# Attention and a gated MLP on one core: the sums of a pair of heads transposed two units later

## The chip, the cores and the metric

The kernel runs on one core of a Trainium2 chip. The metric is device time in microseconds (us) of the whole kernel; lower is better. TensorE (PE) multiplies and transposes; VectorE (DVE), ScalarE (ACT) and GpSimd (POOL) work on elements; SyncE (SP) issues the transfers. Each engine carries out its own list of instructions in order, and semaphores between the engines say when an instruction may start.

## The reference, cut to what matters

```python
def _attn_ref(q, k, v):                       # 4 batches, 8 heads, 576 rows, 64 columns
    scores = scale * np.matmul(q, k.transpose(0, 1, 3, 2))
    mask = block_i >= block_j                 # blocks of 64 rows
    scores = np.where(mask, scores, -1000000000.0)
    scores = scores - np.max(scores, axis=-1, keepdims=True)
    attn = np.exp(scores)
    attn = attn / (np.sum(attn, axis=-1, keepdims=True) + 1e-09)
    return np.matmul(attn, v)
def _moe_ref(x, w_in, w_spatial, b_spatial, w_out):
    h = np.maximum(x @ w_in, 0.0)
    u, v = (h[..., :d_ff // 2], h[..., d_ff // 2:])
    v_n = (v - mu) / np.sqrt(var + 1e-06)     # mean and variance of v's rows
    v_s = np.einsum('ts,bsd->btd', w_spatial, v_n) + b_spatial[None, :, None]
    return (u * v_s) @ w_out
def _moe2_ref(x, g_ln, w_ch1, w_ch2):
    xn = (x - mu) / np.sqrt(var + 1e-06) * g_ln
    return x + np.maximum(xn @ w_ch1, 0.0) @ w_ch2
```

The output of the attention goes through the gated MLP and then through the second MLP, which adds its input.

## The kernel before

**Pairs and units.** The 4 x 8 heads are taken as 16 pairs of heads of one batch, numbered from 0; four pairs make a batch. A pair is worked off in nine units (UNITS). Unit 0 is the tail: the last 64 query rows of both heads, which see all 576 keys. Units 1 and 2 are the fourth block of 128 query rows of each head (four blocks of keys), units 3 and 4 the third (three), 5 and 6 the second (two), 7 and 8 the first (one).

**A unit.** scores(u) multiplies q and k on PE into a bank of the pool p_sc (rows L268 to L308 of the profile). softmax(u) takes the masked maximum on DVE (L323, with L327 for the tail's two parts) and the exponential on ACT (L330), which adds up each row's sum into a column of the tile sm. Two units later (D = 2) transposes(u) turns the unnormalized weights p by 128 x 128 blocks on PE (L380, "tr", as many as there are blocks of keys; the tail has five, in two banks) into a bank of the pool p_tr, which has **two** banks. put copies them to the tiles pH (units of three and four blocks and the tail; by DVE L372, some three-block ones by ACT L374) or pL (the small units; by ACT L374). A bank of p_tr is free for the next taker when this copy is done.

**A pair's end.** Because of the two units' delay, the end of pair p-1 lies in the first units of pair p. At i == 0, unit 7 of p-1 is transposed and reciprocals(p - 1) follows; at i == 1 unit 8; at i == 2 the tail of p itself, and weighted(p - 1, 0), the product of pL with v (L431, "pv<-pL") in a bank of the pool p_mm, which has three. The product with pH, weighted(p, 1), comes in the pair itself at i == 7. reciprocals adds 1e-9 to the sums (L340, DVE), inverts them (L341, DVE), transposes the 128 x 9 tile to nine rows (L343, PE, "rps", a bank of p_tr), copies it (L345, ACT, "rr") and sends it to DRAM and back spread over 64 partitions each ("rb", SP's transfers). store_x, at i == 5, multiplies xx, the copy of the products, by rb (L441, POOL) and splits the result into a high and a low part, xT (L60, L444).

**What else runs there.** While the pairs run, decode_in prepares the MLP's weights (L88 ACT; L89, L90 DVE; L101, L102 POOL, "win"), and prepare casts and splits the next pair's q and k (L58 ACT; L243, L245 POOL, "stack"). From the fifth pair on, fill puts matmuls of the first MLP for finished batches between the units: the value half ("vps", L106 to L108, followed by ACT's vr and DVE's BN_STATS, L112) and the gate half ("ups"). The written order is not the final one: a scheduler reorders each engine's list when the program is built, by its own estimate of the times.

After attention (from about 280 us) come the mixing over rows, the output product and the second MLP, which the change doesn't touch.

Of the kernel before, what the change touches and what calls it, by code (L numbers as in the profile page):

```python
# [8 lines left out]
F32 = mybir.dt.float32  # L9
# [24 lines left out]
def tile_kernel(  # L34
# [26 lines left out]
    NB, NP, _, _, _, S = qk.shape  # L61
# [7 lines left out]
    NPAIR = NB * NP  # L69
# [62 lines left out]
    p_mm = tc.alloc_tile_pool(name="p_mm", bufs=PLAN["mm"], space=PSUM, side="left")  # L132
    p_sc = tc.alloc_tile_pool(name="p_sc", bufs=PLAN["sc"], space=PSUM, side="right")
    p_tr = tc.alloc_tile_pool(name="p_tr", bufs=PLAN["tr"], space=PSUM, side="right")
# [12 lines left out]
    def load(p):  # L147
        if p >= NPAIR:
            return
        b, hp = divmod(p, NP)  # L150
        if p >= PACKED or p % 2 == 0:
            both[:] = [at.tile([128, 2, 2, S], F32, tag="qkt", name="qkt")]
        raw = both[0] if p >= PACKED else both[0][:, p % 2:p % 2 + 1]
        for half in range(2):
            rows = slice(64 * half, 64 * half + 64)
            for j in (0,) if p < PACKED else range(2):
                for x in range(2):
                    h = half if p < PACKED else j
                    nc.sync.dma_start(out=raw[rows, j, x], in_=qk[b, hp, :, h, x])
        nat[p] = raw  # L160

    def load_v(p):
        if p >= NPAIR:
            return
        vts[p] = at.tile([128, 5, 128], F32, tag="vt", name="vt", bufs=3)
        last_load[:] = [nc.sync.dma_start(out=vts[p], in_=v[divmod(p, NP)])]
# [8 lines left out]
    def warm(n):  # L175
        for _ in range(n):
            pin(MM(idle, lhsT=zeros.to_broadcast([128, 128]), rhs=zeros.to_broadcast([128, 512]), start=True, stop=True))
# [136 lines left out]
    def softmax(u):  # L314

        j, c = UNITS[u % NU]
        banks = state[u]
        sm = sums[u // NU]
        pt = tail if c == 4 else at.tile([128, 512], F32, tag="p", name="p", bufs=PLAN['pt'])
        nm = at.tile([128, 2], F32, tag="nm", name="nm", bufs=4)  # L320
        for i, (s_ps, o, n) in enumerate(banks):
            m = mask[:, 0:n] if c == 4 else mask[:, 512 - n:512]
            nc.vector.tensor_tensor_reduce(  # L323
                pt[:, o:o + n], s_ps[:, :n], m, -0.125, 3e38, ALU.add, ALU.min, nm[:, i:i + 1]
            )
        if c == 4:
            nc.vector.tensor_tensor(nm[:, 0:1], nm[:, 0:1], nm[:, 1:2], op=ALU.min)  # L327
        n = o + n
        col = 8 if c == 4 else 4 * j + c
        nc.scalar.activation(  # L330
            pt[:, :n], pt[:, :n], AF.Exp, bias=nm[:, 0:1], scale=-1.0, accum_out=sm[:, col:col + 1]
        )
        state[u] = (pt, n)
# [3 lines left out]
    def reciprocals(p):  # L337

        sm = sums.pop(p)
        nc.vector.tensor_scalar(sm, sm, 1e-9, None, op0=ALU.add)  # L340
        nc.vector.reciprocal(sm, sm)  # L341
        ps = p_tr.tile([128, 512], F32, tag="tr", name="rps")
        nc.tensor.transpose(ps[:9, :128], sm, idn)  # L343
        rr = at.tile([128, 128], F32, tag="rr", name="rr", bufs=1)
        (nc.vector.tensor_copy if p == NPAIR - 1 else nc.scalar.copy)(rr[:9], ps[:9, :128])  # L345
        nc.sync.dma_start(out=r_d[p, :, 0:512].rearrange("j (c q) -> j c q", q=128), in_=rr[:8])
        nc.sync.dma_start(out=r_d[p, :, 512:S], in_=rr[8:9])
        rb = at.tile([128, S], F32, tag="rb", name="rb")
        for j in range(2):
            nc.sync.dma_start(out=rb[64 * j:64 * j + 64], in_=r_d[p, j].partition_broadcast(64))  # L350
        rb_t[p] = rb
# [13 lines left out]
    def transposes(u):  # L365
        j, c = UNITS[u % NU]
        pt, n = state.pop(u)

        def put(src, dst):
            out = dst(pT_of(u // NU)[1 if c >= 2 else 0])  # L370
            if u >= NS - NU or c >= PLAN["ev1" if u >= NU * NP else "ev0"] and not (c == 4 and PLAN["tl1" if u >= NU * NP else "tl0"] == "s"):
                nc.vector.tensor_copy(out, src)  # L372
            else:
                nc.scalar.copy(out, src)  # L374

        def flip(k0, k1):
            tr = p_tr.tile([128, 512], F32, tag="tr", name="tr")
            for kc in range(k0, k1):
                o = 128 * (kc - k0)
                nc.tensor.transpose(tr[:, o:o + 128], pt[:, 128 * kc:128 * kc + 128], idn)  # L380
            return tr

        if c == 4:
            tr = flip(0, 4)
            put(
                tr.rearrange("p (r h q) -> p r h q", h=2, q=64),
                lambda t: view(t, 256, [[WH, 4], [5 * WH, 2], [1, 64]]),
            )
            tr = flip(4, 5)
            put(tr[:, 0:128].rearrange("p (h q) -> p h q", q=64), lambda t: t[:, :, 4 * WH + 256:5 * WH])  # L390
        else:
            tr = flip(0, c + 1)
            put(
                tr[:, :n].rearrange("p (r q) -> p r q", q=128),
                lambda t: view(
                    t, (5 * WH if c >= 2 else 2 * WL) * j + 128 * (c % 2), [[WH if c >= 2 else WL, c + 1], [1, 128]]
                ),
            )
# [5 lines left out]
    def tick():  # L404
        for e in list(slow):
            e[0] -= 1
            if e[0] <= 0:
                slow.remove(e)
                e[1]()

    def flush():
        todo, later[:] = list(later), []
        for f in todo:
            f()

    def weighted(p, part):

        flush()
        vt = ops[p][2]
        if p not in xx_t:  # L420
            xx_t[p] = at.tile([128, S], F32, tag="xx", name="xx")
        xx = xx_t[p]

        jobs = ((0, 128, 0, WL), (1, 128, 128, WL)) if part == 0 else (
            (0, 128, 0, WH), (1, 128, 0, WH), (2, 128, 0, WH), (3, 128, 128, WH), (4, 128, 256, WH))
        w = WH if part else WL
        src = pT_of(p)[part]
        ps = p_mm.tile([128, 512], F32, tag="mm", name="pv")
        for n, (kc, rows, a, z) in enumerate(jobs):
            for j in (1, 0):  # L430
                MM(  # L431
                    ps[64 * j:64 * j + 64, a:z], lhsT=vt[:rows, kc, 64 * j:64 * j + 64],
                    rhs=src[:rows, j, w * kc + a:w * kc + z],
                    start=(n == 0), stop=(n == len(jobs) - 1),
                )
        later.append(lambda: cp('xe', None, xx[:, 256 * part:256 * part + w], ps[:, :w]))

    def store_x(p):
        b, hp = divmod(p, NP)
        xx = xx_t.pop(p)  # L440
        E('xm', p).tensor_tensor(xx, xx, rb_t.pop(p), op=ALU.mult)  # L441
        c0 = (b % 2) * S
        cp('xh', p, xT[0][:, hp, c0:c0 + S], xx)
        E('xl', p).tensor_tensor(xT[1][:, hp, c0:c0 + S], xx, f32(xT[0][:, hp, c0:c0 + S]), op=ALU.subtract)  # L444
        del ops[p]
# [112 lines left out]
    D = PLAN['D']  # L558
    WARM = {2: 5, 3: 2, 4: 2, 5: 1}
    DECODE = {1, 7, 12, 17, 22, 38, 42, 46, 50}  # L560
    for u in range(NS + 8):
        p, i = divmod(u, NU)
        if u < NS:
            scores(u)
            warm(WARM.get(u, 0))
            softmax(u)
        tick()
        flush()
        if D <= u < NS + D:
            transposes(u - D)  # L570
        if i == PLAN['wd'] and p < NPAIR:
            weighted(p, 1)
        if i == 0 and 1 <= p <= NPAIR:
            reciprocals(p - 1)
        if i == D and 1 <= p <= NPAIR:
            weighted(p - 1, 0)
        if i == D + 3 and 1 <= p <= NPAIR:
            store_x(p - 1)
        if i == 0:
            for q in range(2, PACKED) if p == 0 else range(max(p + 2, PACKED), p + 3):  # L580
                load(q)
            load_v(p + 2)
            if p + 1 < NPAIR:
                preps[0] = prepare(p + 1)
        if 0 in preps and i >= 1:
            next(preps[0], None)
        if u in DECODE:
            next(dec, None)
        if p >= NP:
            b, k = divmod(u, NU * NP)  # L590
            if b == 1 and k < 2:
                if k == 0:
                    ahead_of_x = w_in_stage(0)
                next(ahead_of_x)
            if k == PLAN['dstart'] and b <= NB - 1:
                dense = chain(dense, ahead_of_x if b == 1 else w_in_stage(b - 1))
            fill(PLAN['rate'] * size[i] / tot)
# [592 lines left out]
```

## Time and profile before

| | |
|---|---|
| time, median of 3 runs | 803.19 us (801.56 to 804.18) |
| profiled execution, its own time | 804.05 us |
| its span | 802.3 us |
| busy: PE / DVE / ACT / POOL | 98% / 65% / 53% / 52% |
| PE's share of the chain that ended last | 87% |

The span runs from the first to the last instruction of the profiled execution; its own time is 1.75 us longer. A share is that of the whole span. An engine that is busy 98% of it can hardly have more than 2% taken from its waits.

### The profile page before, as it was taken

What the parts mean: (1) busy time and instruction counts of PE and PEld (TensorE: products, weight loads), DVE (VectorE), ACT (ScalarE), POOL (GpSimd) and SP (SyncE); (2) the same over time, 40 slices, a digit from 0 to 9 for tenths busy, and PEclk for the clock granted to TensorE, in tenths of its full rate; (3) what the DMA queues carried; (4) which work ended last, traced back from release to release, by engine and by line L of the source; (5) the groups of instructions that cost most, each with busy time, mean ns of one, the idle gap of its engine ahead of it and who ended that gap; (6) DMA issues with size and microseconds to landing.
All of it is one profiled execution on the core that took longest, in us unless ns stands there. A gap on an engine that the chain in (4) does not pass through costs nothing.

```text
span 802.3 us, 13325 instructions
## 1 busy us (share of the span) xinstructions
PE 782.6 (98%) x4504; PEld 669.7 (83%) x4508; DVE 521.3 (65%) x1184; ACT 428.6 (53%) x1080; POOL 418.5 (52%) x435
## 2 busy tenths in 40 slices
PE   9989899999999999999999999999999999999998
PEld 4667688878888799889988889888889888888986
DVE  6667655665555277877677787897566588645534
ACT  4776677677675264555354554553354454433421
POOL 4598865765462352233285465555545465445431
PEclk9999999999999999999999999999999999999999
DMA  9855454446242468788420342204001003000002
GB/s 253 194 154 166 125 158 137 123 142 189 67 150 73 139 211 279 224 265 279 160 93 1 102 135 79 80 0 158 1 21 34 0 1 125 21 1 1 1 1 78
DMA packets 53848, 88.70 MB, mean 111 GB/s; under 512 B 6931, under 2 KB 17299, under 8 KB 53781
## 3 DMA queue, kind: packets, MB, share of 16 engines
q1 hardware_dynamic: 53540, 87.55, 36.4%
q8 instruction: 35, 0.57, 0.3%
q10 hardware_dynamic: 240, 0.31, 0.2%
q14 instruction: 33, 0.26, 0.1%
HBM read 68.88 MB, written 18.95 MB: 109 GB/s over the span
## 4 chain that ended last, share of the span: by engine, by line
PE 87%; DVE 6%; DMA 3%; ACT 2%; issue 1%; POOL 1%; SPq 0%; POOLq 0%; DVEq 0%; ACTq 0%
PE hps L969 21%; PE o L106 8%; PE o L108 8%; PE o L107 8%; PE pv L431 6%; PE tr L380 5%; PE sc L308 4%; PE ups L106 2%; PE ups L108 2%; PE ups L107 2%; PE vps L106 2%; DMA raw<-in_w_ch_dram 2%; PE vps L107 2%; PE vps L108 2%; PE sc L302 2%; PE sc L286 2%
## 5 line engine op out<-in xcount | busy, mean ns | idle before, releaser
L102 POOL TENSOR_TENSOR a<-s,a 128x256 fp32r<-128x256 f32 x96 | 78.3, 820 | 93.0 <-ACT a L97 93.0
L107 PE MATMUL o<-w,h 128*128 128x512 f32 x288 | 112.9, 393 | 0.0
L106 PE MATMUL o<-w,h 128*128 128x512 f32 x288 | 107.8, 398 | 1.0 <-ACT h L961 1.0
L975 DVE TENSOR_TENSOR c<-hps,c 128x384 f32<-128x384 f32 x120 | 66.5, 554 | 54.6 <-PE hps L969 53.0
L108 PE MATMUL o<-w,h 128*128 128x512 f32 x288 | 97.5, 397 | 0.1
L323 DVE CUSTOM_DVE_ANT_0 p<-sc,mask 128x512 f32<-128x512 f32 (+3 forms) x128 | 58.5, 478 | 50.5 <-PE sc L308 27.0
L330 ACT ACTIVATE p<-p,nm 128x512 f32<-128x512 f32 (+3 forms) x128 | 71.1, 556 | 28.7 <-DVE nm L323 27.6
L102 POOL TENSOR_TENSOR a<-w,a 128x256 fp32r<-128x256 f32 x72 | 61.0, 850 | 44.4 <-ACT a L97 38.6
L97 ACT CAST a<-s 128x256 fp32r<-128x256 f32 x96 | 38.4, 404 | 84.3 <-PE hps L969 76.1
L372 DVE COPY pH<-tr 128x512 f32<-128x512 f32 (+1 forms) x88 | 49.6, 574 | 32.8 <-PE tr L380 32.1
L106 PEld LDWEIGHTS o<-w,h 128*128 128x128 f32 x288 | 53.7, 188 | 11.8 <-ACT h L961 2.3
L107 PEld LDWEIGHTS o<-w,h 128*128 128x128 f32 x288 | 54.1, 188 | 10.1
L108 PEld LDWEIGHTS o<-w,h 128*128 128x128 f32 x288 | 53.2, 188 | 8.8 <-DVE h L962 1.0
L380 PE MATMUL tr<-idn,p 128*128 128x128 f32 x320 | 55.0, 279 | 4.2 <-DVE pH L372 4.0
L819 POOL TENSOR_TENSOR gt<-gf,gt 128x576 fp32r<-128x576 f32 (+1 forms) x17 | 25.0, 1471 | 61.1 <-ACT gt L818 61.1
L380 PEld LDWEIGHTS tr<-idn,p 128*128 128x128 f32 x320 | 37.7, 140 | 14.2 <-DVE pH L372 6.2
L117 POOL TENSOR_TENSOR rs<-rs,nhalf 128x1 f32<-128x1 f32 x36 | 22.4, 623 | 49.4 <-DVE rs L116 44.4
L962 DVE SCALAR_TENSOR_TENSOR h<-c,h 128x384 fp32r<-128x384 f32 x72 | 46.5, 665 | 1.5 <-ACT h L961 1.5
L243 POOL TENSOR_TENSOR stack<-qkt,stack 64x576 fp32r<-64x576 f32 x24 | 34.5, 1439 | 23.5 <-ACT stack L58 19.2
L88 ACT ACTIVATE dm<-raw 128x256 f32<-128x256 f32 (+1 forms) x72 | 32.1, 462 | 26.9 <-DVE w L90 9.2
L308 PE MATMUL sc<-stack 128*128 128x512 f32 (+3 forms) x192 | 43.7, 340 | 1.8 <-DVE nm L323 1.4
L441 POOL TENSOR_TENSOR xx<-xx,rb 128x576 f32<-128x576 f32 x16 | 22.8, 1425 | 41.0 <-DMA rb<-r_d 18.1
(188 smaller groups left out, 2286.0 us busy)
## 6 DMA issues: line engine op xcount, KB each, us to landing
raw<-in_w_ch_dram SPq DMA_DIRECT2D x64, 256.0 KB
qkt<-in_qk_dram SPq DMA_DIRECT2D x110, 144.0 KB
vt<-in_v_dram SPq DMA_DIRECT2D x16, 320.0 KB
rb<-r_d SPq DMA_DIRECT2D x32, 144.0 KB
u_d<-ur SPq DMA_DIRECT2D x16, 288.0 KB
us<-u_d SPq DMA_DIRECT2D x16, 288.0 KB
y_d<-ys SPq DMA_DIRECT2D x18, 256.0 KB
yr<-y_d SPq DMA_DIRECT2D x18, 256.0 KB
```

Of the source, the lines that this page charges most:

```text
L102: {"v": nc.vector, "g": nc.gpsimd}[low].tensor_tensor(lo, src, f32(hi), op=ALU.subtract)
L106: MM(out_ps, lhsT=a[0], rhs=b[0], start=first, stop=False)
L107: MM(out_ps, lhsT=a[0], rhs=b[1], start=False, stop=False)
L108: MM(out_ps, lhsT=a[1], rhs=b[0], start=False, stop=last)
L308: MM(s_ps[:, :nn], lhsT=st[:, j, i, q], rhs=st[:, j, 2, 0:nn], start=(i == 0), stop=(i == 1))
L323: nc.vector.tensor_tensor_reduce(pt[:, o:o + n], s_ps[:, :n], m, -0.125, 3e38, ALU.add, ALU.min, nm[:, i:i + 1])
L330: nc.scalar.activation(pt[:, :n], pt[:, :n], AF.Exp, bias=nm[:, 0:1], scale=-1.0, accum_out=sm[:, col:col + 1])
L372: nc.vector.tensor_copy(out, src)
L380: nc.tensor.transpose(tr[:, o:o + 128], pt[:, 128 * kc:128 * kc + 128], idn)
L431: MM(ps[64 * j:64 * j + 64, a:z], lhsT=vt[:rows, kc, 64 * j:64 * j + 64], rhs=src[:rows, j, w * kc + a:w * kc + z], start=(n == 0), stop=( ...
L969: MM(ps, lhsT=a[x], rhs=b[y], start=not more and kc == 0 and k == 0, stop=kc == KD // 2 - 1 and k == 2, skip_group_check=True,)
L975: nc.vector.tensor_tensor(out, ps, x, op=ALU.add)
```

## The change

For all pairs but 3 and 15, reciprocals moves from i == 0 to i == 2, behind weighted(p - 1, 0), and store_x from i == 5 to i == 7. Pairs 3 and 15 keep their places. Pair 3's rps takes its bank from p_mm and no longer from p_tr.

```diff
@@ -339,7 +339,10 @@
         sm = sums.pop(p)
         nc.vector.tensor_scalar(sm, sm, 1e-9, None, op0=ALU.add)
         nc.vector.reciprocal(sm, sm)
-        ps = p_tr.tile([128, 512], F32, tag="tr", name="rps")
+        if p == NP - 1:
+            ps = p_mm.tile([128, 512], F32, tag="mm", name="rps")
+        else:
+            ps = p_tr.tile([128, 512], F32, tag="tr", name="rps")
         nc.tensor.transpose(ps[:9, :128], sm, idn)
         rr = at.tile([128, 128], F32, tag="rr", name="rr", bufs=1)
         (nc.vector.tensor_copy if p == NPAIR - 1 else nc.scalar.copy)(rr[:9], ps[:9, :128])
@@ -570,11 +573,14 @@
             transposes(u - D)
         if i == PLAN['wd'] and p < NPAIR:
             weighted(p, 1)
-        if i == 0 and 1 <= p <= NPAIR:
+        urgent = p - 1 in (NP - 1, NPAIR - 1)
+        if i == 0 and 1 <= p <= NPAIR and urgent:
             reciprocals(p - 1)
         if i == D and 1 <= p <= NPAIR:
             weighted(p - 1, 0)
-        if i == D + 3 and 1 <= p <= NPAIR:
+            if not urgent:
+                reciprocals(p - 1)
+        if i == D + (3 if urgent else 5) and 1 <= p <= NPAIR:
             store_x(p - 1)
         if i == 0:
             for q in range(2, PACKED) if p == 0 else range(max(p + 2, PACKED), p + 3):
```

All engines issue the same instructions as before; what changes is their order, in attention alone. In the lists below a row is an instruction or a run of equal ones (x11 is eleven), with the line of its own version (L343 before is L346 now, L380 is L383, L431 is L434).

First PE at the end of pair 2, where no filler stands; stack_90 and stack_89 are q and k of pair 3. Before:

```order
L302 MATMUL sc<-stack_90 128x256 x6
L343 MATMUL rps<-idn,sm 9x128
L380 MATMUL tr<-idn,p 128x128
L302 MATMUL sc<-stack_90 128x192 x3
...
L286 MATMUL sc<-stack_89,qtail_87 128x256 x4
L380 MATMUL tr<-idn,tail 128x128 x5
L431 MATMUL pv<-pL,vt 64x256 x2
L431 MATMUL pv<-pL,vt 64x128 x2
L380 MATMUL tr<-idn,p 128x128 x11
L286 MATMUL sc<-stack_89,qtail_87 128x320 x4
```

And now:

```order
L302 MATMUL sc<-stack_90 128x256 x6
L383 MATMUL tr<-idn,p 128x128
L383 MATMUL tr<-idn,tail 128x128 x4
L302 MATMUL sc<-stack_90 128x192 x3
...
L286 MATMUL sc<-stack_89,qtail_87 128x256 x4
L383 MATMUL tr<-idn,tail 128x128
L434 MATMUL pv<-pL,vt 64x256 x2
L434 MATMUL pv<-pL,vt 64x128 x2
L346 MATMUL rps<-idn,sm 9x128
L383 MATMUL tr<-idn,p 128x128 x11
```

The transpose of the sums has gone from ahead of unit 8's single block to just ahead of the eleven blocks of units 1, 2 and 3; four of the tail's five blocks stand right behind unit 8 now. Pairs 1, 7 and 9 read alike.

Then PE at the end of pair 4, from the product with pL on; the vps are filler. Before:

```order
L431 MATMUL pv<-pL,vt 64x128 x2
L380 MATMUL tr<-idn,p 128x128 x4
L108 MATMUL vps<-win_82,xT_85 128x512 x2
L380 MATMUL tr<-idn,p 128x128 x4
L106 MATMUL vps<-win_82,xT_84 128x512
...
L108 MATMUL vps<-win_82,xT_85 128x512
L380 MATMUL tr<-idn,p 128x128 x3
L286 MATMUL sc<-stack_89,qtail_87 128x320 x4
L380 MATMUL tr<-idn,p 128x128 x3
L308 MATMUL sc<-stack_89 128x512 x4
```

And now:

```order
L346 MATMUL rps<-idn,sm 9x128
L383 MATMUL tr<-idn,p 128x128 x4
L106 MATMUL vps<-win_82,xT_84 128x512
...
L108 MATMUL vps<-win_82,xT_85 128x512 x3
L383 MATMUL tr<-idn,p 128x128 x7
L286 MATMUL sc<-stack_89,qtail_87 128x320 x4
L383 MATMUL tr<-idn,p 128x128 x3
L308 MATMUL sc<-stack_89 128x512 x4
L383 MATMUL tr<-idn,p 128x128 x4
```

Between units 1 and 2 (four blocks each) stood two vps and stand fourteen now; unit 2's blocks join unit 3's three, and two of the small units' blocks come earlier. On DVE in the same place, before:

```order
L372 COPY pH<-tr 128x4x128
L323 ISA p,nm<-sc,mask 128x128
L323 ISA nm 128x1
L372 COPY pH<-tr 128x4x128
L323 ISA p,nm<-sc,mask 128x128
...
L112 BN_STATS st<-vr 128x6
```

And now:

```order
L375 COPY pH<-tr 128x4x128
L323 ISA p,nm<-sc,mask 128x128
L323 ISA nm 128x1
L112 BN_STATS st<-vr 128x6
L375 COPY pH<-tr 128x4x128
```

BN_STATS stands between the copies of units 1 and 2. Last, POOL from the end of pair 2 to that of pair 3; the stack tiles hold q and k of the coming pairs. Before:

```order
L444 TENSOR_TENSOR xT_85<-xx,xT_84 128x576
L243 TENSOR_TENSOR stack_89<-qkt,stack_89 64x576
L245 TENSOR_TENSOR stack_89<-qkt,stack_89 64x576
L101 TENSOR_SCALAR win_82<-dm 128x512
L243 TENSOR_TENSOR stack_89<-qkt,stack_89 64x576
```

And now:

```order
L447 TENSOR_TENSOR xT_85<-xx,xT_84 128x576
L101 TENSOR_SCALAR win_82<-dm 128x512
L243 TENSOR_TENSOR stack_89<-qkt,stack_89 64x576
L245 TENSOR_TENSOR stack_89<-qkt,stack_89 64x576
L102 TENSOR_TENSOR win_83<-dm,win_82 128x512
```

The cast of the weights has moved ahead of the two subtractions.

## Rows read from the trace of the kernel before

**Rows 1.** The page: span, busy time of each engine, the chain that ended last.

```profile
span 802.3 us, 13325 instructions
...
PE 782.6 (98%) x4504; PEld 669.7 (83%) x4508; DVE 521.3 (65%) x1184; ACT 428.6 (53%) x1080; POOL 418.5 (52%) x435
...
PE 87%; DVE 6%; DMA 3%; ACT 2%; issue 1%; POOL 1%; SPq 0%; POOLq 0%; DVEq 0%; ACTq 0%
```

**Rows 2.** Windows: stretch, length, busy PE, PEld, DVE, ACT, POOL; granted clock, DMA.

```profile
0.00:100.00 100.00, 91.70 (x560) 61.57 (x564) 68.38 (x206) 66.62 (x192) 72.86 (x74) 0.98 0.67 179
100.00:280.00 180.00, 176.53 (x1227) 147.37 (x1226) 96.71 (x324) 117.08 (x320) 96.04 (x96) 1.00 0.44 131
280.00:802.00 522.00, 514.32 (x2721) 460.78 (x2720) 356.24 (x655) 244.90 (x569) 249.63 (x265) 1.00 0.29 90
...
92.00:95.00 3.00, 1.39 (x7) 0.55 (x5) 3.00 (x11) 0.37 (x1) 2.80 (x4) 1.00 0.43 111
95.00:99.00 4.00, 4.00 (x22) 2.02 (x21) 1.77 (x8) 2.88 (x8) 3.91 (x6) 0.57 0.82 211
```

**Rows 3.** PE's waits, 10 to 280 us: us in total, times, longest.

```profile
PE tr L380 <- DVE pH L372: 4.0, 9, 1.3
PE rps L343 <- ACT pL L374: 2.0, 2, 1.2
...
PE vps L108 <- POOL xT L444: 0.5, 1, 0.5
```

**Rows 4.** PE's timeline, ends of pairs 2 and 9: start, duration, wait ahead in brackets.

```profile
53.45 0.28 PE L343 MATMUL rps<-idn,sm 128*9 128x128 f32 x1 [0.79 <-ACT pL L374]
...
57.56 1.09 PE L380 MATMUL tr<-idn,p 128*128 128x128 f32 x8
59.00 0.55 PE L380 MATMUL tr<-idn,p 128*128 128x128 f32 x3 [0.34 <-DVE pH L372]
...
175.23 0.55 PE L380 MATMUL tr<-idn,p 128*128 128x128 f32 x3 [0.35 <-DVE pH L372]
```

**Rows 5.** DVE's timeline, end of pair 2, the copies of units 1 and 2.

```profile
58.25 0.69 DVE L372 COPY pH<-tr 128x512 f32<-128x512 f32 x1 [0.61 <-PE tr L380]
...
59.07 0.69 DVE L372 COPY pH<-tr 128x512 f32<-128x512 f32 x1
```

**Rows 6.** ACT's timeline, end of pair 2.

```profile
53.03 0.53 ACT L374 COPY pL<-tr 128x256 f32<-128x256 f32 x2
```

**Rows 7.** PE's timeline, ends of pairs 3 and 4.

```profile
72.35 0.55 PE L380 MATMUL tr<-idn,p 128*128 128x128 f32 x3 [1.31 <-DVE pH L372]
...
82.40 0.28 PE L343 MATMUL rps<-idn,sm 128*9 128x128 f32 x1 [1.20 <-ACT pL L374]
```

**Rows 8.** DVE's timeline, 70 to 81 us.

```profile
70.01 1.69 DVE L90 SCALAR_TENSOR_TENSOR dm<-dm,de 128x512 uint32<-128x512 uint32 x1
...
75.27 1.38 DVE L340 TENSOR_SCALAR sm<-sm 128x9 f32<-128x9 f32 x1
...
80.57 0.68 DVE L90 SCALAR_TENSOR_TENSOR dm<-dm,de 128x512 uint32<-128x512 uint32 x1
```

**Rows 9.** POOL's timeline, 69 to 77 us.

```profile
69.63 1.51 POOL L243 TENSOR_TENSOR stack<-qkt,stack 64x576 fp32r<-64x576 f32 x1 [1.76 <-ACT stack L58]
...
75.14 1.48 POOL L245 TENSOR_TENSOR stack<-qkt,stack 64x576 fp32r<-64x576 f32 x1
```

**Rows 10.** PE's timeline, end of pair 4, 89 to 99 us.

```profile
89.47 0.39 PE L106 MATMUL vps<-win,xT 128*128 128x512 f32 x1
89.69 0.39 PE L107 MATMUL vps<-win,xT 128*128 128x512 f32 x1
...
94.53 0.62 PE L308 MATMUL sc<-stack 128*128 128x384 f32 x2 [1.44 <-DVE nm L323]
```

**Rows 11.** DVE's timeline, end of pair 4.

```profile
88.76 0.69 DVE L112 BATCH_NORM_STATS2 st<-vr 128x6 f32<-128x512 f32 x1
...
94.40 0.55 DVE L372 COPY pH<-tr 128x384 f32<-128x384 f32 x1
```

## The prediction, as it was recorded

> **What bounds the kernel now.** I began with the page: TensorE (PE) is busy 98% of the span and makes up 87% of the chain that ended last [rows 1]. So a change can gain only what PE idles, and can lose whatever new wait it puts on PE. The windows say where the idle time lies: 8.30 us of the first 100 us, 3.47 of the next 180 and 7.68 of the last 522, where attention is over and the order of every engine is the same before and after [rows 2]. What can move is thus within some 12 us, all of it in the pair loop. The chain then shows what stands behind PE's gaps there: VectorE (DVE) 6%, ScalarE (ACT) 2%.
>
> Next I read PE's waits by line. Two of them are of the instruction that the change moves, the transpose of the sums (rps): 2.0 us in all. Nine are of transposes that wait for DVE's copy of an earlier transpose to pH: 4.0 us [rows 3]. Last I went to the places, pair by pair, in the timeline of PE and of the engine that it waits for.
>
> One look at the clock: from 95 to 99 us the granted clock is 0.57 of full speed (a mean over both levels), and before it PE was busy for only 1.39 of 3.00 us [rows 2]. That fall costs (1 - 0.57) x 4.00 = 1.7 us.
>
> **The change, part by part.** Every engine issues the same instructions as before; 14 of 16 pairs have rps, the copy rr and the r DMAs later, and xx*rb two units later. So the sum has only waits in it.
>
> *The two waits of rps, 0.79 and 1.20 us* [rows 4, 7]. What rps waits for is a bank of p_tr: the bank is free when ACT has copied the transposes of unit 6 to pL. At 53.03 ACT copies units 6 and 7 in one run, 0.53 us for both, behind six exponentials [rows 6], and rps starts when the first is done. In the new order the next instruction on PE is unit 8's transpose, and it needs the same bank. It is reached just as early, since rps no longer stands ahead of it, and it waits for the same copy. Wait passed on: 0 us. The bounds are 0 and -2.0, the latter if the copy came for some other reason 1.2 us sooner.
>
> *A new wait behind rps, pairs 1, 2, 7 and 9.* p_tr has two banks. Before, the two 4-block transposes (units 1 and 2) ran back to back, 8 blocks in one go at 57.56 [rows 4], because two banks were free; the third taker, unit 3, waited for the copy of unit 1: 0.34 us at 59.00, 0.35 at 175.23 [rows 4]. Now rps stands just ahead of unit 1 and takes a bank. Unit 1 takes the other (that of tail block 4, copied long before), and unit 2 gets that of unit 1, which DVE must first copy: in these pairs the built program has unit 2 wait for unit 1's copy, and rps's own bank goes to unit 3. So PE meets the same copy one unit sooner. Unit 2's transposes (4 blocks; 8 show 1.09 with the last one's drain, which is 8 x 0.11 = 0.88 when they follow one another, so 0.44) no longer run within that copy. DVE's copy starts at 58.25 and takes 0.69, and it can't be earlier, since unit 1's transposes are not: rps's own 0.2 us left one place above and came in here [rows 4, 5]. New wait 0.34 + 0.44 = 0.8 instead of 0.34: +0.45 for each of the four, **+1.8 us**. Bounds: 0, if unit 3 and what follows had to wait for something later anyway, and +2.8, if unit 2's own copy, now 0.6 us later than 59.07, holds unit 3's successor for another 0.25 each.
>
> *Pair 3's rps in a p_mm bank.* Pair 3 keeps its time; only its bank differs, and the two 4-block transposes find both p_tr banks as free as before. What changes here is a by-product, the order on GpSimd (POOL): L101, the cast of the weights, now comes before the two big subtractions of the stack, L243 and L245, where before it came after. Beside L243 (69.63 to 71.14) DVE's L90 took 1.69 us, beside nothing such 0.68 [rows 8, 9]; the copies to pH stood behind it, and PE waited 1.31 at 72.35 [rows 7]. If L90 now runs free of L243, up to 1.0 us of that wait goes (1.69 - 0.68). But the stall only feeds the next one: DVE's L340 takes 1.38 beside L245 [rows 8, 9], and its chain of exponentials and copies ends in the 1.20 us wait at 82.40 [rows 7]. What PE gains at 72 it would mostly wait longer at 82. I take **-0.3**, bounds -1.0 and 0.
>
> The Trainium skill (SBUF — State Buffer, section "Who interferes with whom") states that VectorE and GpSimd share a pair of ports as an exclusive lock. That L90 took 1.69 us beside POOL's subtraction and 0.68 without agrees with it. By that rule alone the gain at 72 us would be the whole 1.0, and the sum +2.1 instead of +2.8.
>
> *Pair 4 (82 to 99 us).* Here filler exists: value matmuls (vps) of the first batch, which step 0.23 us each, 0.39 in duration [rows 10]. Before, 2 of them stood between units 1 and 2, and 12 behind; now 14 stand between (14 x 0.23 = 3.2 us), because the scheduler fills the wait that it foresees for unit 2. On DVE BN_STATS of a value tile moves ahead of unit 2's copy and the last scores' reduction and copy stand no earlier. What ended the gap of 1.44 us at 94.53 was DVE's reduction, and its copy at 94.40 ended at 94.95 [rows 10, 11]. With unit 2 and all behind it on DVE some 3 us later and one of 0.69 (BN_STATS, 88.76 [rows 11]) ahead of it, I estimate the end of that run 1.5 to 2.6 us later, with 0.6 of PE work (units 6, 7) drawn ahead of the gap. I take **+1.0**; bounds -1.6 (the gap vanishes) and +2.6.
>
> *Pairs 0, 5, 6, 8, 10 to 14.* In all but pair 0 some 14 vps or ups (the gate's matmuls) stand between units 1 and 2 now, 3.2 us, so that unit 1's copy (0.69) or rr's is done when unit 2 comes. These matmuls stood behind unit 2 before and covered its copy, which now comes straight before unit 3; 0.35 of cover at most is lost in each, as in [rows 4]. That is 8 x 0.35 = 2.8 if every cover was needed. But nine such waits in all, four of them in the pairs above, made only 4.0 us [rows 3]. I take **+0.3**, bounds 0 and +2.
>
> *The later xx*rb and xT.* The only PE wait on xT is 0.5 us [rows 3]. xT is needed by the next stage eight units into the next batch, and two units are some 3 us. The pairs that end a batch are 3, 7, 11, 15; 3 and 15 are kept early, 7 and 11 are not. Value 0, since PE idles only 3.47 us from 100 to 280 us and for xT once; the bound is +1 (that wait again at both).
>
> Sum: 0 + 1.8 - 0.3 + 1.0 + 0.3 + 0 = **+2.8 us**. The profiled execution took 804.05 us, 1.75 of it outside the span, so by its own time 806.9. It stands 0.86 above the median of the runs shown, 803.19, so I carry the sum to that: **806.0**.
>
> **The rivals.**
> *Faster: the DVE run of pair 4 no longer stalls PE.* The place is 92 to 99 us: 1.6 us of idle and the 1.7 us clock fall behind it [rows 2]. With 14 vps ahead of units 2 to 4 instead of behind, PE may have work until DVE is through; then both vanish, -3.3. With pair 3's -1.0 and the four new waits at +1.8 (not avoided: the bank decides) this is 803.2 - 2.5 = 800.7. It decides if unit 4's copy in pair 4 ends no later, in PE's own order, than the vps that are in front. For it: the filler now stands ahead of the DVE run. Against: the filler is the same amount, and the DVE copies that release PE are behind it too.
> *No change to be measured.* The copies of unit 1 are exposed by less than I think (say 0.2 each, +0.8) and pair 4 comes out even: 804. A measurement of this kernel can tell some 0.3%, 2.4 us, from no change, so every sum from -2.4 to +2.4 falls here. For it: the mechanism moves PE's waits and none is above 1.44 us. That the waits of rps simply pass to unit 8's transpose is this case too.
> *Clearly slower.* The clock falls a second time, as it did behind 92 to 95 us, since PE's idle time at 40 to 80 us comes in larger pieces; and the dense pairs lose their cover: 2.8 + 1.7 + 1.7 (their bound less what I took) = 6.2, 809.4. Against it: at 44 to 73 us PE had waits of 1.31 us without a fall.
>
> **How the numbers follow.** The sum's case and the rival of a second fall both end slower: 0.32 and 0.10, 0.42 by more than 0.3%. No change 0.38, faster 0.20. The likeliest is the sum, 806.0. The range goes from 800.5 (the faster rival, with something over) to 810.5 (the slow one with 1.1 for pairs 7 and 11); it leaves out less than 2 in 10. The forecast's own range is 803.5 to 808.
>
> **What would show it.** Right: rps nowhere waits more than a few tenths; unit 8's transpose (one block) waits 0.8 and about 1.2 us near 53 and 82 us, for ACT's pL; in pairs 1, 2, 7 and 9 four transposes in place of eight, then a wait of some 0.8 us for pH; L90 near 70 us at about 0.7 us. Wrong: PE's idle time of the first 100 us falls below 6.3, that is, the rps waits are gone rather than moved; or the clock stays full through 95 to 99 us; or a wait of some size on rr's copy or on xT.

## The result

The changed kernel took 810.15 us (median of 6 runs, 808.0 to 813.76), the kernel before 803.68 us beside it: a ratio of 1.0087 (95% interval 1.0064 to 1.0111). That is 6.5 us, more than twice the forecast of +2.8. A second series of the same kernel gave 1.0066 (1.0041 to 1.0090).

The profiled execution spans 810.5 us, 8.2 more than that of before; by its own time, 812.30 us, it is 2.15 above the median of its series. The page of the changed kernel: span, busy time, the chain that ended last.

```profile
span 810.5 us, 13317 instructions
...
PE 785.2 (97%) x4508; PEld 670.2 (83%) x4508; DVE 519.0 (64%) x1184; ACT 429.7 (53%) x1080; POOL 416.7 (51%) x435
...
PE 78%; DMA 7%; DVE 5%; ACT 4%; POOL 3%; issue 2%; SPq 1%; ACTq 0%; POOLq 0%; DVEq 0%
```

The windows, as in [rows 2] (attention ends some 2.8 us later), and ten us of a later stage, where before shows 10.00 us busy at a clock of 1.00:

```profile
0.00:100.00 100.00, 91.86 (x561) 61.33 (x562) 67.15 (x204) 66.07 (x189) 69.01 (x70) 0.98 0.67 179
100.00:283.00 183.00, 177.64 (x1229) 146.87 (x1229) 94.89 (x328) 119.44 (x325) 99.25 (x102) 1.00 0.43 129
283.00:810.00 527.00, 515.70 (x2721) 462.00 (x2719) 356.94 (x655) 244.22 (x568) 248.46 (x265) 1.00 0.29 90
340.00:350.00 10.00, 7.78 (x48) 7.58 (x47) 8.29 (x22) 6.81 (x17) 2.42 (x3) 0.83 0.70 222
```

The chain gives PE 9 points less and DMA 4 more than [rows 1]. The first two windows lose about 0.2 less and 1.9 more of idle time than in [rows 2]; the last is the surprise: 527 us in place of 522, for the same instructions in the same order, 11.3 us idle in place of 7.7. Going through PE's timeline by equal instructions: the last product with pH starts at 262.93 against 260.11 (+2.8), the transposes of yn (the second MLP's input) at 342.54 against 338.44 (+4.1), a later first-layer matmul at 546.15 against 539.08 (+7.1). So attention lost what the sum had said, and the stages that the prediction had set aside lost 4.3 more; the last 1.1 us stand behind the last matmul, where the output is written.

PE's waits from 10 to 290 us, as in [rows 3]; then its timeline at the places of [rows 4, 7]:

```profile
PE tr L383 <- ACT pL L377: 4.4, 5, 1.5
PE tr L383 <- DVE pH L375: 4.3, 8, 0.8
...
PE vps L108 <- POOL xT L447: 0.3, 1, 0.3
```

```profile
53.59 0.33 PE L383 MATMUL tr<-idn,p 128*128 128x128 f32 x1 [0.79 <-ACT pL L377]
60.63 0.98 PE L383 MATMUL tr<-idn,p 128*128 128x128 f32 x7 [0.78 <-DVE pH L375]
74.35 0.55 PE L383 MATMUL tr<-idn,p 128*128 128x128 f32 x3 [0.35 <-DVE pH L375]
84.78 0.33 PE L383 MATMUL tr<-idn,p 128*128 128x128 f32 x1 [1.49 <-ACT pL L377]
...
239.82 0.33 PE L383 MATMUL tr<-idn,tail 128*128 128x128 f32 x1 [0.99 <-ACT pL L377]
```

The first and fourth rows are rps's old waits of 0.79 and 1.20, now unit 8's, at 0.79 and 1.49. The second is the new wait in front of units 2 and 3, 0.78 where 0.34 stood. The third is pair 3's, 0.35 where 1.31 stood. The last has no row before.

**Behind attention.** DVE's timeline near 340 us, first of before, then of after: the decoding of a weight tile (L89) stands ahead of the statistics of yn, and waits for the tile's transfer 0.52 us before and 1.86 after.

```profile
336.44 0.30 DVE L89 TENSOR_SCALAR raw<-raw 128x256 uint32<-128x256 uint32 x1 [0.52 <-DMA raw<-in_w_ch_dram]
336.65 0.18 DVE L114 BATCH_NORM_AGGREGATE mv<-st 128x2 f32<-128x6 f32 x1
...
471.60 0.69 DVE L112 BATCH_NORM_STATS2 st<-yn 128x6 f32<-128x512 f32 x1 [0.74 <-DMA yn<-y_d]
```

```profile
340.54 0.29 DVE L89 TENSOR_SCALAR raw<-raw 128x256 uint32<-128x256 uint32 x1 [1.86 <-DMA raw<-in_w_ch_dram]
340.75 0.17 DVE L114 BATCH_NORM_AGGREGATE mv<-st 128x2 f32<-128x6 f32 x1
...
478.62 0.69 DVE L112 BATCH_NORM_STATS2 st<-yn 128x6 f32<-128x512 f32 x1 [2.20 <-DMA yn<-y_d]
```

PE's transposes of yn wait for it, first before, then after:

```profile
338.44 0.63 PE L752 MATMUL ytr<-idn,yn 128*128 128x128 f32 x4 [0.88 <-DVE yn L122]
```

```profile
342.54 1.08 PE L758 MATMUL ytr<-idn,yn 128*128 128x128 f32 x4 [2.22 <-DVE yn L122]
```

The granted clock falls behind that: 0.83 over ten us (a mean over both levels), which costs (1 - 0.83) x 10 = 1.7 us. The last row of either DVE list is the second place: yn's way back from DRAM, with a wait of 0.74 us before and 2.20 after. What differs there is who else uses the DMA engines. The DMA part of one microsecond, 466 to 467 of before and 475 to 476 of after (queue, kind: packets, MB, share of 16 engines):

```profile
q8 instruction: 1, 0.02, 6.5%
```

```profile
q8 instruction: 1, 0.02, 10.7%
```

This is a code load, the transfer that brings the next block of PE's instructions while the kernel runs. One such packet occupies one of the 16 DMA engines for 6.5% x 16 = 1.0 us, in after 1.7. SP issues yn's two transfers, first before, then after:

```profile
468.92 2.32 SPq L767 DMA_DIRECT2D yn<-y_d  x2
```

```profile
474.45 2.19 SPq L773 DMA_DIRECT2D yn<-y_d  x2
```

Before, the load (466.5) is over by then; after, it (475.3) falls among them. The load has moved because the built program has 16 semaphore instructions fewer on PE (4364 instructions against 4380, where a multiplication and its weight load mostly count as one), all of them in pairs 4 to 14, as the two halves below show: each block of PE's code is wanted that much later in the work.

### The profile page after: what moved, and what is told of

Same layout as the page of the kernel before. It is cut to its first block, busy times and chain, and to the rows that moved or that the text cites. A ratio compares the mean times of both kernels' runs of the same rounds, so it can differ in the third digit from the quotient of the medians.

```text
span 810.5 us, 13317 instructions
## 1 busy us (share of the span) xinstructions
PE 785.2 (97%) x4508; PEld 670.2 (83%) x4508; DVE 519.0 (64%) x1184; ACT 429.7 (53%) x1080; POOL 416.7 (51%) x435
## 4 chain that ended last, share of the span: by engine, by line
PE 78%; DMA 7%; DVE 5%; ACT 4%; POOL 3%; issue 2%; SPq 1%; ACTq 0%; POOLq 0%; DVEq 0%
PE hps L975 21%; PE o L106 8%; PE o L108 8%; PE o L107 8%; PE pv L434 4%; PE tr L383 4%; PE sc L308 2%; PE ups L106 2%; PE ups L108 2%; PE ups L107 2%; DMA raw<-in_w_ch_dram 2%; PE sc L302 2%; PE by L106 2%; PE by L107 1%; PE by L108 1%
## 5 line engine op out<-in xcount | busy, mean ns | idle before, releaser
L383 PE MATMUL tr<-idn,p 128*128 128x128 f32 x320 | 55.7, 281 | 7.7 <-DVE pH L375 4.3
L383 PEld LDWEIGHTS tr<-idn,p 128*128 128x128 f32 x320 | 37.0, 140 | 19.4 <-DVE pH L375 9.0
L117 POOL TENSOR_TENSOR rs<-rs,nhalf 128x1 f32<-128x1 f32 x36 | 22.6, 631 | 48.5 <-DVE rs L116 39.5
L967 ACT ACTIVATE h<-c 128x384 fp32r<-128x384 f32 x72 | 35.3, 521 | 16.5 <-DVE c L981 16.2
```

## The experiments

**The same again, and the two halves of the change.**

```diff
e1_after_again, e2_before_again: nothing altered
e3_move_early
-        urgent = p - 1 in (NP - 1, NPAIR - 1)
+        urgent = p - 1 in (NP - 1, NPAIR - 1) or p > NP
e4_move_late
+        urgent = p - 1 in (NP - 1, NPAIR - 1) or p <= NP
```

> The changed kernel once more, with nothing altered, for a second profile. Up to 331 us the first profile of after is 2.8 us behind that of before, and 8.2 at the end. Theory A (the rest is part of the change: attention ends later, and the stages behind it meet their weight transfers at another phase): the second profile again shows at least 1.5 us of wait of the transpose of yn near 340 us and some 7 us of PE idle behind 285 us, 806 to 808 of span where the clock stays full. Theory B (the rest is what one execution happened to have: a clock fall at 342 us, a slow transfer): PE's idle behind 285 us is back at about 5, and the time comes near 806.5.

> The kernel before once more, nothing altered, for a second profile and as a control. Both theories: a ratio of 1.000 within 0.3%, PE idle behind 285 us of about 5 us, the stall before 95 us with a clock fall of 1.7 us behind it. If the idle time behind 285 us differs by 2 us from the first profile, that is what one execution differs from another by, and theory B gains.

> The move for pairs 0 to 2 alone, with pair 3's sums in the bank of the products; pairs 4 to 14 as before. By my sum: two new bank waits (pairs 1 and 2, 0.45 each) less 0.3 of pair 3, that is +0.6 us, and the stall of pair 4 (1.4 us at 94 us) as before. If the clock fall that the first profile of after showed at 55 to 60 us comes from these waits, it repeats: +1.7 more. Rival, the harm is all in the early pairs: +4 or more.

> The move for pairs 4 to 14 alone, with pair 3's sums in the bank of the products; pairs 0 to 2 as before. By my sum: two bank waits (pairs 7 and 9, 0.9 us), pair 4 +1.0, the rest +0.3, pair 3 -0.3: +1.9 us. By theory A (attention's end meets the later stages at another phase) most of the change's +6.5: +4 to +5.5. Rival, the harm is all in the early pairs: within 1 us of before.

The changed kernel: 1.0066 (1.0041 to 1.0090). Its second profile repeats the waits behind attention, 2.48 us for yn and 0.79 near 485 us (0.81 in the first), and the clock fall, so theory B fell. The kernel before: 1.0011 (0.9995 to 1.0026), with 1.08 us for yn. Its stall of [rows 10] is there again, 1.45 us at 96.60, but not the clock fall that I had expected behind it; that stands at 55 to 60 us:

```profile
55.00:60.00 5.00, 5.00 (x26) 3.56 (x26) 0.89 (x2) 3.31 (x7) 4.86 (x4) 0.66 0.51 149
96.60:100.60 4.00, 4.00 (x29) 2.71 (x30) 2.24 (x9) 2.88 (x9) 3.79 (x7) 1.00 0.84 220
```

So a fall, worth (1 - 0.66) x 5 = 1.7 us, changes its place in attention between executions of one program. The early half: 1.0013 (0.9998 to 1.0028), waits behind attention as before. The late half: 1.0028 (1.0010 to 1.0047), 2.2 us, near my sum's +1.9, but not by its way: in its profile attention ends 4.1 us *sooner* than in that of before (no clock fall in it), and yet it has the long waits, 1.92 us for yn and 0.82 near 477, and a clock fall behind the first. So it isn't a later end of attention that makes them (theory A as I had put it); it is something that the move in pairs 4 to 14 brings and that outlives attention. The two halves differ in PE's instruction count: 4380 with the early half, 4364 with the late.

**PE's code loads.** Idle matmuls of zeros at the kernel's start change where every later load of PE's code falls, and nothing else of the program but the start (in the two runs on before with 240 and 248, a few instructions of the first microseconds).

```diff
e5_after_pad16, e14_after_pad16_again (after)
     warm(10)
+    warm(8, 64)           # 8 matmuls of 64 columns: 16 instructions with their weight loads
e13_after_pad72 (after)
-    warm(10)
+    warm(6)
+    warm(40, 52)
e6_before_pad240, e15_before_pad248 (before)
-    warm(10)
+    warm(130, 32)         # e15: 134
e9_before_pad56, e10_before_pad112 (before)
-    warm(10)
+    warm(6)               # e10: 2
+    warm(32, 64)          # e10: 64
```

> The changed kernel with 8 more idle matmuls of 64 columns (16 instructions of PE with their weight loads) behind the ten at the start, where PE waits 0.81 us for a transfer; nothing else differs. The changed program has 16 semaphore instructions fewer on PE than before, and its code loads come 2 to 4 us later against the work. Theory C (the later code loads of PE collide with the weights and with y's way through DRAM): the wait for yn falls from 2.2 to about 1.0 us, those near 480 us from 1.5 to 0.2, the clock stays full at 340 to 350 us, and the kernel comes at about 805 to 806, 2 to 3 us behind before. Rival (attention's later end, or its order, makes the later stages slow): the waits stay at 2.2 to 2.5 and 1.5 us, and the time at 808.5 to 810.

> The kernel before with 130 idle matmuls of 32 columns at the start in place of ten of 512: 240 instructions more on PE, which is 16 short of the 256 that lie between two of its code loads, so that these stand where they stand in the changed kernel; the rest of the program is as before. Theory C: the wait for yn near 340 us grows from 0.9 to some 2.2 us, waits of 1.2 to 1.5 us come up near 475 us, and the time is 2.5 to 4 us above before, if the start itself costs nothing. Rival: the waits behind 285 us are as before (4.3 to 4.9 us in all), whatever the start makes of the time.

The kernel before with 240 instructions more: 1.0067 (1.0041 to 1.0093), 4.0 us by the medians. The order of its attention is that of before and its start costs nothing (the first product with pH at 20.29 us against 20.58). Its profiled execution is the fastest of its six, with no clock fall in attention, which ends 2.2 us sooner than in that of before. PE's waits behind 288 us in it, its window from 335 to 340 us, and DVE's two waits for transfers:

```profile
PE ytr L752 <- DVE yn L122: 2.5, 1, 2.5
PE o L106 <- ACT h L961: 1.6, 4, 0.8
```

```profile
335.00:340.00 5.00, 3.35 (x15) 3.38 (x16) 3.75 (x13) 2.92 (x8) 1.36 (x2) 0.66 0.39 134
```

```profile
334.66 0.30 DVE L89 TENSOR_SCALAR raw<-raw 128x256 uint32<-128x256 uint32 x1 [2.20 <-DMA raw<-in_w_ch_dram]
...
472.12 0.69 DVE L112 BATCH_NORM_STATS2 st<-yn 128x6 f32<-128x512 f32 x1 [1.68 <-DMA yn<-y_d]
```

Both waits and the clock fall (0.66) of the changed kernel stand here in the old program, with a code load at 469.3 us, 0.8 behind the issue of yn's transfers at 468.49. The other way round, 16 instructions more in the changed kernel gave 1.0049 (1.0033 to 1.0066): no wait above 0.23 us near 480, 1.57 for yn in place of 2.2 to 2.5, no clock fall behind attention. So the waits at both places went the way of theory C, in both directions, the first of them only in part (1.57 against 0.88 and 1.08 in before). At the second place the load is seen at work: in the four profiles in which DVE waits 1.7 us or more there (both of the changed kernel, e4, e6), a load begins 0.8 to 1.2 us behind the issue of yn's transfers, and in no other profile here does one.

At the first place it is not seen. In the changed kernel and in e6 the load (333.4 and 327.8 us) is over before SP issues the weight tile with another (335.53 and 329.88; 332.20 in before), and from there to the decoding it is 5.0 and 4.8 us against 4.2, less than the wait grew by. That the changed start makes this wait longer, e6 shows; by which way stays open. What theory C does not explain is the 3.8 us that are left.

> The kernel before with 6 idle matmuls of 512 columns and 32 of 64 at the start in place of ten of 512: 56 instructions more on PE, so that each code load comes 56 of PE's instructions (some 6 us of matmuls of 0.23) earlier in the work; the rest is as before. Theory C: only the waits that a load runs into change; those behind 285 us differ from before's 4.3 us by up to 2.5 either way, and the time by -1 to +3. Rival (the 240 of the other run harmed by the changed start, not by the loads): the waits behind 285 us are as before.

> The same with 2 idle matmuls of 512 columns and 64 of 64 at the start: 112 instructions more on PE. Theory C: as for 56, another set of waits behind 285 us. Rival: waits as before, the time as that of the run with 56.

1.0002 (0.9986 to 1.0018) and 1.0000 (0.9986 to 1.0013), with 0.92 and 1.62 us for yn and no wait above 0.23 near 480: most places of the loads are harmless, and so is a changed start.

> The kernel before with 134 idle matmuls of 32 columns at the start in place of ten of 512, 248 more instructions on PE, half the shift of the run with 240. Theory C: the load near 467 us stands between where it harmed (470) and where it didn't (466), so its wait may be either; the one near 338 us grows to between 0.9 and 2.5. The time lies between 0 and +4 us. Rival (the changed start, not the loads, did the harm with 240): as with 240, +4 us, with the same waits of 2.5 and 0.8.

1.0029 (1.0009 to 1.0049): 1.15 us for yn, nothing above 0.23 near 480 (the load stands at 470.3, 0.2 us behind the issue of yn's transfers, and DVE waits 0.79 us for them), two clock falls before 100 us. Half the shift, less than half the harm by the ratios, though their intervals overlap; the waits of e6 are gone with almost the same start, so the rival that the start is to blame falls.

**What is left: the order in attention.**

> The changed kernel with 6 idle matmuls of 512 columns and 40 of 52 at the start in place of ten of 512: PE then has 4436 instructions, as the kernel before with 56 more, in which code loads cost nothing. Theory C: what is left is the order in attention; the waits behind 285 us are about 5 us as there, and the time is 2 to 3 us above before (four bank waits of 0.44, and the tail's wait for pL). Rival (the order in attention costs next to nothing, all of it is where the loads stand): within 1 us of before.

> The changed kernel with 8 more idle matmuls at the start, once more for a second profile and more runs, beside the same at 72: if the order in attention is what is left, both are alike, at a ratio of 1.002 to 1.005; the wait of the tail's transpose for pL near 239 us, absent in its first profile, is there or not. If the loads still weigh in attention, the two differ by more than 1.5 us.

1.0062 (1.0041 to 1.0082) and 1.0061 (1.0041 to 1.0080), both above what I had expected. With two more sets of load places the loss stays, so some 4 to 5 us (e5 with them) go with the order that the change brings, more than my sum. The profiles put less of it into attention itself: it ends 0.5 us (e5), 0.9 (e13, with no clock fall in it where before's has one) and 3.2 (e14) later than in before's, of 1.9, 3.0 and 3.9 in the whole span; the rest, behind attention, is not placed. In both new profiles the largest wait in attention is the tail's transpose at the end of pair 13, 1.65 and 2.81 us; in that of e5 it was absent. I followed it back in the changed kernel (POOL, then ACT):

```profile
234.20 1.43 POOL L444 TENSOR_TENSOR xx<-xx,rb 128x576 f32<-128x576 f32 x1 [4.53 <-ACT p L330]
235.72 0.67 POOL L60 TENSOR_SCALAR xT<-xx 128x576 fp32r<-128x576 f32 x1
236.47 1.43 POOL L447 TENSOR_TENSOR xT<-xx,xT 128x576 fp32r<-128x576 f32 x1
237.85 0.55 POOL L117 TENSOR_TENSOR rs<-rs,nhalf 128x1 f32<-128x1 f32 x1
238.51 0.26 POOL L120 TENSOR_SCALAR nb<-mv,rs 128x1 f32<-128x1 f32 x1
```

```profile
238.81 0.81 ACT L121 ACTIVATE vr<-vr,nb,rs 128x512 f32<-128x512 f32 x1 [2.94 <-POOL nb L120]
239.53 0.24 ACT L377 COPY pL<-tr 128x128 f32<-128x128 f32 x1
```

POOL idles 4.53 us in front of xx*rb, whose last input is rb: SP issued it at 230.50. (The row names an exponential as releaser; a wait for several things is put down to the last by the profile's events, and ACT's p doesn't feed xx. In the second profile of the changed kernel the row names rb.) Behind it in POOL's queue stand L117 and L120, the small steps of a value tile's normalization; behind those, in ACT's queue, L121; behind L121 the copy to pL that empties the bank for the tail. In e5 rb was issued at 228.15 and xx*rb started at 231.92, in e14 at 230.00 and 234.63. Over the whole of attention POOL waits for rb more than twice as long as before (13 waits in place of 3); first before, then after:

```profile
POOL xx L441 <- DMA rb<-r_d: 18.1, 3, 10.8
```

```profile
POOL xx L444 <- DMA rb<-r_d: 42.2, 13, 11.4
```

```diff
e16_pad16_pair12_early (e5 and)
-        urgent = p - 1 in (NP - 1, NPAIR - 1)
+        urgent = p - 1 in (NP - 1, 12, NPAIR - 1)
e17_pad16_bank4 (e5, with warm(5, 64), and)
-        if p == NP - 1:
+        if p in (1, 2, NP - 1, 7, 9):
```

> The changed kernel with 8 more idle matmuls at the start (PE: 4380 instructions, as before), and pair 12's reciprocals at their old place, as those of pairs 3 and 15. Theory D: at the end of pair 13 POOL stands at xx*rb of pair 12, waiting for r's way through DRAM, ahead of the two small operations that ACT's L121 needs; L121 stands ahead of the copy to pL, and PE's transpose of the tail waits for it (0 to 2.8 us in the profiles of the changed kernel). With pair 12's r sent early this wait near 240 us is gone, and the time falls by 1 to 2 us against the same kernel without that. Rival (ACT is late there for its own work): the wait stays at 1 to 2.8 us, no change in time.

> The changed kernel with the sums of pairs 1, 2, 7 and 9 (beside pair 3's) in a bank of the products, and 5 more idle matmuls at the start (PE: 4380 instructions). By my sum the four waits of 0.78 us for the copy of unit 1 go back to 0.35 or less: 1.8 us faster than the changed kernel with 16 added, 2 to 3 us above before. Theory E (a wait for a bank in the dense part costs more than itself, since filler can't pass it): more than 3 us of the loss go, the time within 1 us of before, as with all pairs' sums in that pool. Rival: no change, the waits go elsewhere.

Pair 12 alone put back: 1.0025 (1.0006 to 1.0044), 1.9 and 2.9 us less than e5 and e14 by the ratios, and no wait of the tail near 240 us. Eleven of its twelve times (802.71 to 805.60 us) lie below all six of e14 (806.17 to 810.79). PE's waits for ACT's copies to pL, first e14, then e16:

```profile
PE tr L384 <- ACT pL L378: 6.2, 5, 2.8
PE tr L384 <- DVE pH L376: 4.3, 8, 0.8
```

```profile
PE tr L384 <- DVE pH L376: 4.3, 8, 0.8
PE tr L384 <- ACT pL L378: 3.1, 4, 1.5
```

Theory D held for this kernel; what e7 and e12 say of it stands below. The bank in pairs 1, 2, 7 and 9: 0.9994 (0.9976 to 1.0013), the whole loss gone. Its waits:

```profile
PE tr L384 <- DVE pH L376: 2.3, 7, 0.5
PE tr L384 <- ACT pL L378: 2.2, 3, 1.2
```

The waits for pH fell by 2.0 us, near my sum (four times 0.43 to 0.44, 1.7), and those for pL by 4.0 against e14, the tail's to 0.50. That is Theory E's outcome, but not by its reason: the scheduler built another order (125 of PE's rows, 25 of POOL's differ), in which the tail's wait is short too, so this run doesn't price the bank alone.

**Banks and combinations.**

```diff
e7_all_mm, e12_all_mm_pad6 (after; e12 with warm(3, 64) behind warm(10))
-        if p == NP - 1:
-            ps = p_mm.tile([128, 512], F32, tag="mm", name="rps")
-        else:
-            ps = p_tr.tile([128, 512], F32, tag="tr", name="rps")
+        ps = p_mm.tile([128, 512], F32, tag="mm", name="rps")
e8_bank_only (before; this choice of bank for pair 3, nothing moved)
e11_late_pad16 (e4 with warm(8, 64) behind warm(10))
```

> The changed kernel with the sums of all pairs in a bank of the products (p_mm) and none in p_tr; 6 semaphore instructions fewer on PE than before. By my sum the new bank waits (0.8 us at pairs 1, 2, 7, 9) go back to 0.35: attention ends 1.8 us sooner than in the changed kernel. Theory C: with 6 instead of 16 fewer instructions the code loads lie between the two, so the waits behind 285 us may be either. Rival (the order of units 1 and 2 is the harm): within 1 us of the changed kernel.

> The kernel before with pair 3's sums alone in a bank of the products; nothing moved. By my sum -0.3 us (0 to -1.0), from the order on POOL in pairs 3 and 4. One semaphore instruction more on PE: by theory C the waits behind 285 us are as before. Rival, the gain of move_late in attention (4 us) comes from this bank: 2 to 4 us faster than before.

> The move for pairs 4 to 14 alone (pairs 0 to 2 as before, pair 3 in the bank of the products) with 8 more idle matmuls of 64 columns at the start, which give PE as many instructions as before (4380). Theory C: of that kernel's +1.6 to 2.3 us over before the waits near 334 and 478 us (1.0 and 1.2 more than before) and the clock fall behind them go: within 1 us of before. Rival: unchanged at +1.6 to 2.3.

> The changed kernel with all pairs' sums in the bank of the products, and 3 more idle matmuls of 64 columns at the start, so that PE has as many instructions as before (4380). Theory C: the code loads stand as before, the wait near 340 us falls from 1.7 to about 1, and the kernel gains 0.5 to 1 us on the one without them: 801 to 802, 0 to 1.5 us faster than before. Rival: no difference from the one without them.

All sums in p_mm: 0.9999 (0.9981 to 1.0018), and with before's instruction count 0.9990 (0.9976 to 1.0003). PE's wait for yn is 1.7 us in e7 and still 1.6 in e12, where theory C had expected about 1. In e7 attention ends 1.8 us sooner than in the changed kernel, as my sum has it, and no wait for pH is above 0.4 us. But the tail at the end of pair 13 waits longer than in the changed kernel, 3.53 us in e7 and in e12

```profile
236.33 0.33 PE L381 MATMUL tr<-idn,tail 128*128 128x128 f32 x1 [2.28 <-ACT pL L375]
```

behind the same wait of POOL for rb (4.64 us). So the wait of theory D doesn't by itself make a kernel slower than before; with the sums out of p_tr it is made up for elsewhere. All sums in p_mm with pair 12 early wasn't run.

The bank of pair 3 alone: 1.0007 (0.9995 to 1.0020); its waits at 70.78 and 94.60 us are 0.35 and 0.50 where [rows 7, 10] have 1.31 and 1.44, but that gain doesn't reach the time. The late half with 16 instructions: 1.0009 (0.9993 to 1.0025) in place of 1.0028, and no wait above 0.23 us near 480, as theory C has it; yn still waits 1.66. No version is clearly faster than the kernel before; the best, e12, has 1.000 in its interval. Moving store_x alone wasn't run: the scheduler then builds the same order on every engine as without it, so that part of the diff does nothing.

## Why the prediction was wrong

The direction was right and the size was off: +2.8 forecast, +6.5 measured, with an interval of 5.1 to 8.9 in the first series. Two terms that the prediction put at nothing are shown to have failed; a third may be too small.

- **"What can move is thus within some 12 us, all of it in the pair loop."** This step failed. Behind 283 us I had counted 0, since the order there is the same. In the profiles of the changed kernel these stages lose 1.3 us at yn, 1.7 to a clock fall, and some 1.2 near 480. Putting 16 instructions back brings the ratio from 1.0087 and 1.0066 to 1.0049 and 1.0061, and 240 added to the kernel before cost it 1.0067: so where the code loads fall is shown as a cause. Its share in the changed kernel is only bounded, at 0.4 to 3 us (from 1.0066 to 1.0061, from 1.0087 to 1.0049), and these intervals overlap.
- **"The later xx*rb and xT. Value 0", bound +1.** I had looked at who waits for xT, not at what stands behind xx*rb in POOL's queue. The wait for rb holds L117, L120, ACT's L121 and the copy to pL; with pair 12 alone put back the time fell by 1.9 to 2.9 us.
- **The bank.** With all sums in p_mm, or those of five pairs, and PE's instruction count of before, nothing is left of the loss (0.9990 and 0.9994), where e5 and e14 keep 4 to 5 us. So the bank, with the order that the scheduler builds for it, decides more than the +1.8 that the sum gave it, although the tail's wait stays in e12. What it costs by itself no run shows.
- *The two waits of rps, passed on: 0.* Right: 0.79 and 1.49 us on unit 8's transpose.
- *The new wait, pairs 1, 2, 7, 9: +1.8.* Right in place and size: 0.79, 0.78, 0.78 and 0.78 us for 0.35, 0.34, 0.35 and 0.35, that is +1.7.
- *Pair 3: -0.3.* The wait at 72 us fell by 0.96, all of what L90's 1.69 for 0.68 us would give; at 82 us 0.29 came back.
- *Pair 4: +1.0.* Wrong sign: the stalls of 1.44 and 0.17 at 92 to 95 us became 0.20 and 0.46. The clock fell at 55 to 60 us in place of 95 to 99, as it did in e2, where nothing was changed: the 1.7 us that the prediction counts with this stall are not tied to it. e8, with the bank alone, shows the stall at 0.50 as well, so it goes with pair 3's bank and the order built for it.
- *Rivals.* The slow one (809.4) has the time, and a second clock fall, but at 342 us and not in the pair loop; its reason, dense pairs without cover, wasn't seen.
- *The signs.* Of those of being wrong one came: the clock stays full from 95 to 99 us (1.00). It does so in e2 too (1.00), so it could not tell anything of the change.

In attention the sum and the profile agree at +2.8, by luck: the pieces above make 1.7 + 0.3 - 1.0 - 0.9 + 1.6 (two waits of the tail) = +1.7, and 1.1 us are not placed. Open, too, are the 1.1 us at the very end: from the last matmul's start to the end of the span it is 4.2 us in before, 5.3 to 5.4 in both profiles of the changed kernel, in e14 and in e16, and 4.6 to 4.7 in e5 and e13.

## What to carry to other kernels

An operation that waits for a trip through DRAM, moved later, holds what is queued behind it on its own engine: follow that queue to the next engine, and the next, down to the bank that isn't emptied, and then test what the time pays for it: in e16 it fell with that wait, in e12 the wait stood and was made up for elsewhere. When an edit changes an engine's instruction count, also in semaphores alone, the places of its code loads shift for the rest of the kernel; a few idle instructions at the start tell such a loss from the edit's own. A timing of a small edit is worth little before that control. Profile the unchanged kernel twice: a clock fall of 1.7 us that stands behind a stall in one execution can stand elsewhere in the next.

## What the runs showed of the hardware

The loads of PE's code are visible as one packet each in the DMA part. The page of before counts them:

```profile
q8 instruction: 35, 0.57, 0.3%
```

0.57 MB in 35 packets is 16 KB each, and PE's 4504 + 4508 instructions make 257 per packet. A packet holds one DMA engine 0.9 to 2.1 us in the profiles of before and after. Data transfers issued 0.8 to 1.2 us ahead of one were waited for 1.68 (e6), 1.88 (e4) and 2.20 us (after) where 0.74 stood.

The Trainium skill (Runtime: NRT & Kernel Launch, section "Instruction fetch mechanics") gives blocks of 16 KiB or 256 instructions and calls the cost of a block's boundary mostly hidden. These counts agree with the first. The second holds here for the engine that fetches (ten loads begin between 100 and 280 us of before, where PE idles 3.47 us in all), but not for the transfers beside it: e6 is 0.67% slower (0.41 to 0.93) with only its start changed, and e9 and e10, whose loads fall elsewhere, are not.
